# Tiles 5 to 7 in f16 halves, the scan's end column copied by ScalarE, and a new order of the first 480 entries of an attention and MLP kernel

## The chip, the cores and the metric

The kernel runs on one core of one Trainium2 chip. The metric is the device time of one execution in microseconds (us); of several runs the median is taken. The profile is of one further execution.

## The reference

A gated linear attention over 768 steps, for 4 batches of 8 heads of 48 columns, and a layer of two products with a clipped gate between them, on its 3072 outputs of 384 columns.

```python
f = 1.0 / (1.0 + np.exp(-f_logit))
for t in range(S):
    state = f[:, :, t, :, None] * state + np.einsum('bhd,bhe->bhde', k[:, :, t], v[:, :, t])
    y[:, :, t] = np.einsum('bhd,bhde->bhe', q[:, :, t], state)
...
h = x @ w_in
g = h * np.clip(h + 3.0, 0.0, 6.0) / 6.0
return g @ w_out
```

x is y with its heads side by side; w_in is 384 x 2048, w_out 2048 x 384. All is fp32.

## The kernel before

**Work.** The attention is done in 24 units, one for a batch and a chunk of 128 steps. The four units of one chunk make a group of 512 rows for the layer, and there are six groups. The 2048 hidden columns are 16 tiles of 128. Entry mm2.18, for example, is the second product of group 1 (18 = 16 + 2), tile 2.

**A unit.** SP loads its gate logits (`load`, into one of three buffers), its q and k (`loadq`, 512 KB) and v (`loadv`, 200 KB). ScalarE takes the sigmoid (`gate`). VectorE scans the gates backward (`back`, L428), multiplies k by the result (`kmul`, L441), takes the column at which each chunk's scan ends, `sf[:, :, 0]`, and its reciprocal (`rend`: L444 a maximum with a small limit into `ends`, L445 the reciprocal of it), scans forward from the reciprocal over the same buffer (`fwd`, L448), and multiplies q (`qmul`, L454). TensorE transposes k (`tk`, L516), ScalarE copies it out (`ktok`), TensorE makes the update of the state (`kv`, L537), the scores (`att`, L497) and the outputs (`qs`, L571, and `av`, L587). VectorE masks the scores (`mask`, L504), multiplies the old state by `ends` (`decay`, L457) and adds (`carry0`, `carry1`). ScalarE rounds the outputs to f16 into `xmem` (`xh`); TensorE subtracts the rounded part (`xs`) and ScalarE takes the remainder (`xl`), in the first group; a DMA fills the rows between heads (`hole`).

**A weight tile.** SP loads 768 KB (`ld`, into one of three buffers `raws`). ScalarE makes an integer part and a short of its top (`z`, L288; `cy`, L297), VectorE trims, moves and joins it into `wide` (`mid` L301, `dif` L308, `top` L312), ScalarE rounds to f16 (`high`, L317), and the remainder is a subtraction in whole or in halves for w_in and w_out (`low`, `lowi`, `lowo`, L320).

**A tile of the layer.** The first product is nine f16 matmuls of 512 columns: rounded times rounded, remainder times rounded and rounded times remainder, for three blocks of rows (`mm1`, L664). ScalarE makes the clipped part (`relu`), VectorE the gate product (`g`, L678). The second product has two forms. In one it takes g in fp32 and the fp32 weights in `wide`: three matmuls (`mm2x`, L720; for tiles 0 to 4 of group 0 the two halves of 256 rows apart, `mm1a`, `ga`, `mm2a` and so on, L828 to L846). In the other ScalarE rounds g to f16 (`gh`, L683), VectorE or GpSimd takes its remainder (`gl`, L693), and nine f16 matmuls follow (`mm2`, L709). Group 0 uses the fp32 form for tiles 0 to 7, since these come before the remainders of w_out.

**Order.** The program is recorded by walking through a list of entries, `ORDER`; each engine and each DMA queue runs its own instructions in that order. `warm.N` is N idle matmuls of 128 columns on TensorE. A digit after the second dot names a PSUM bank. `ON_POOL` lists the entries that go to GpSimd and not to VectorE. A DMA on SP waits until the one eight before it has landed.

The lines that the change touches:

```python
def turn():
    nc.vector.tensor_scalar_max(ends[:, i], sf[:, :, 0], END_LIMIT)
    nc.vector.reciprocal(rend[:, :, 0], ends[:, i])
def engine(op, i):
    return nc.gpsimd if f"{op}.{i}" in ON_POOL else nc.vector
```

## Time and profile before

| what | us |
|---|---|
| runs shown, three | 458.67, 458.91, 459.29 |
| median | 458.91 |
| the profiled execution | 459.1 |
| its span, first to last instruction | 457.4 |
| TensorE busy | 449.4 |
| VectorE busy | 359.3 |
| ScalarE busy | 231.2 |
| GpSimd busy | 19.0 |

Busy time counts an engine's instructions where at least one runs. Matmuls overlap, and the recorded duration of one goes on to the modelled end of its pipeline. Idle time of an engine stands with what released it. In the stretches that the tables use, the first 480 entries of the list run from the start to about 114 us.

### The profile page before, as it was taken

How to read it: one execution, taken by the hardware profiler on the slowest of the kernel's cores; microseconds unless marked ns; L12 is line 12 of the kernel's file. 1: busy time of each engine (PE TensorE's matmuls, PEld its weight loads, DVE VectorE, ACT ScalarE, POOL GpSimd, SP SyncE). 2: the span in 40 equal slices, each digit the busy share in tenths (PEclk: the TensorE clock that was granted, in tenths of full speed). 3: DMA queues.
4: the chain of work that ended last, by engine and by line, in shares of the span. 5: the costliest groups of instructions: out<-in, count | busy, mean ns of one | idle time of the engine just before them, and what ended most of it. 6: DMA issues, size and time to landing. Idle time of an engine off the chain costs nothing.

```text
span 457.4 us, 12555 instructions
## 1 busy us (share of the span) xinstructions
PE 449.4 (98%) x5445; PEld 292.8 (64%) x5449; DVE 359.3 (79%) x643; ACT 231.2 (51%) x389; POOL 19.0 (4%) x31
## 2 busy tenths in 40 slices
PE   8899999999999999999999999999999999999996
PEld 4578755544455556685767666676676757677764
DVE  6999999979999999989886764888683676466562
ACT  3776777765454445554455265245263443442531
POOL 3000211131000000000000000000000000000000
PEclk9999999999999999999999999999999999999999
DMA  8669656640142512303202240040000010030002
GB/s 283 223 251 385 225 189 251 203 155 16 52 125 99 158 52 59 108 3 120 89 1 85 78 142 18 21 143 2 1 10 1 5 29 2 1 115 2 1 0 73
DMA packets 25531, 43.18 MB, mean 94 GB/s; under 512 B 2560, under 2 KB 17408, under 8 KB 25472
## 3 DMA queue, kind: packets, MB, share of 16 engines
q1 hardware_dynamic: 23872, 41.56, 27.0%
q8 instruction: 43, 0.70, 0.6%
q10 hardware_dynamic: 1600, 0.79, 0.6%
q14 instruction: 16, 0.13, 0.1%
HBM read 36.43 MB, written 4.72 MB: 90 GB/s over the span
## 4 chain that ended last, share of the span: by engine, by line
PE 94%; DVE 2%; DMA 1%; ACT 1%; issue 0%; SPq 0%; ACTq 0%
PE o L709 35%; PE pair L772 16%; PE single L772 9%; PE pair L664 7%; PE single L664 5%; PE o L846 3%; PE pair L497 3%; PE pair L587 3%; PE pair L571 3%; PE pair L537 2%; PE o L720 2%; PE pair L516 2%; PE o_half L862 1%; PE pair L862 1%; PE single L828 1%; PE pair L828 1%
## 5 line engine op out<-in xcount | busy, mean ns | idle before, releaser
L709 PE MATMUL o<-gg,weight 128*128 128x512 f16 x744 | 173.5, 379 | 0.1
L709 PEld LDWEIGHTS <-weight 128*128 128x128 f16 x744 | 71.7, 98 | 73.8
L772 PEld LDWEIGHTS <-weight 128*128 128x128 f16 x672 | 65.1, 98 | 13.3 <-issue 0.2
L772 PE MATMUL pair<-xmem,wide 128*128 128x256 f16 x384 | 51.2, 273 | 0.1
L683 ACT ACTIVATE gg<-raws 128x512 f16<-128x512 f32 x64 | 38.4, 624 | 23.9 <-DVE raws L806 8.1
L772 PE MATMUL single<-xmem,weight 128*128 128x256 f16 x384 | 49.8, 273 | 0.2 <-DVE raws L806 0.2
L801 ACT ACTIVATE raws<-pair,half 128x512 f32<-128x512 f32 x32 | 21.5, 684 | 42.7 <-PE pair L772 33.7
L772 PEld LDWEIGHTS <-wide 128*128 128x128 f16 x384 | 36.9, 98 | 8.7 <-DVE single L787 0.6
L801 ACT ACTIVATE raws<-single,half 128x512 f32<-128x512 f32 x32 | 22.0, 687 | 40.0 <-PE single L772 32.4
L664 PEld LDWEIGHTS <-weight 128*128 128x128 f16 x243 | 23.1, 98 | 26.8 <-issue 0.3
L772 PE MATMUL pair<-xmem,weight 128*128 128x256 f16 x288 | 36.5, 273 | 0.0
L806 DVE SCALAR_TENSOR_TENSOR raws<-raws,single 128x512 f32<-128x512 f32 x32 | 21.8, 682 | 18.4 <-ACT raws L801 18.4
L693 DVE TENSOR_TENSOR gg<-raws,gg 128x512 f16<-128x512 f32 x48 | 31.9, 682 | 5.0 <-ACT gg L683 5.0
L664 PE MATMUL pair<-xmem,weight 128*128 128x512 f16 x144 | 33.2, 379 | 0.0
L787 DVE TENSOR_TENSOR pair<-pair,raws 128x512 f32<-128x512 f32 x16 | 11.2, 697 | 25.5 <-PE pair L772 17.2
L806 DVE SCALAR_TENSOR_TENSOR raws<-raws,pair 128x512 f32<-128x512 f32 x32 | 21.5, 681 | 12.3 <-ACT raws L801 12.1
L448 DVE TENSOR_TENSOR_SCAN suffix<-gates,rend 112x516 f32<-112x516 f32 x24 | 29.7, 1236 | 0.1
L428 DVE TENSOR_TENSOR_SCAN suffix<-gates,unit 112x516 f32<-112x516 f32 x23 | 28.1, 1224 | 0.5 <-ACT gates L422 0.5
L664 PE MATMUL single<-xmem,weight 128*128 128x512 f16 x99 | 23.2, 380 | 0.1
L674 ACT ACTIVATE tg<-pair,half 128x512 f32<-128x512 f32 x16 | 10.9, 687 | 19.5 <-PE pair L664 16.3
L683 ACT ACTIVATE gg<-tg 128x512 f16<-128x512 f32 x24 | 14.4, 626 | 9.1 <-DVE tg L678 5.2
L504 DVE TENSOR_TENSOR a<-pair,causal 128x512 f32<-128x512 f32 x24 | 16.3, 682 | 1.2 <-PE pair L537 1.2
(133 smaller groups left out, 641.6 us busy)
## 6 DMA issues: line engine op xcount, KB each, us to landing
qkf<-qk SPq DMA_DIRECT2D x24, 512.0 KB, 4.9
raws<-w SPq DMA_DIRECT2D x16, 768.0 KB, 6.0
gates<-fg SPq DMA_DIRECT2D x23, 258.5 KB, 3.8
v<-v SPq DMA_DIRECT2D x24, 200.0 KB, 3.8
outT<-os SPq DMA_DIRECT2D x11, 256.0 KB, 3.1
outT<-os SPq DMA_DIRECT2D x8, 128.0 KB, 1.9
wide<-wide SPq DMA_DIRECT2D x32, 24.0 KB, 2.0
outT<-os ACTq DMA_DIRECT2D x2, 256.0 KB, 4.1
```

The lines of the kernel that those rows point to most:

```text
L428: nc.vector.tensor_tensor_scan(flat(sf)[:, ::-1], gt[:, 1:][:, ::-1], flat(unit)[:, ::-1], 0.0, op0=ALU.mult, op1=ALU.add,)
L448: nc.vector.tensor_tensor_scan(flat(sf), gt[:, :NP * (C + 1)], flat(rend), 0.0, op0=ALU.mult, op1=ALU.add,)
L497: nc.tensor.matmul(d["at"][HC * odd:HC * (odd + 1), e, 2 * n + c], t[rs, 1, n, c, odd], t[rs, 0, n, c, odd], start=not growing[at], stop=T ...
L504: nc.vector.tensor_tensor(d["a"].rearrange("r p e t -> r e p t"), d["at"], causal.unsqueeze(1).unsqueeze(1).broadcast_to([128, 2, NP, HC]) ...
L571: nc.tensor.matmul(d["y"][to:to + 64, odd, n, cs], before[rs, p], t[rs, 0, n, c, odd], start=alone and (odd, e) not in seen, stop=False, s ...
L664: nc.tensor.matmul(h, win[:, f, a, k * 128:(k + 1) * 128], g["xt"][:, k, :g["n"] // C, b], start=i == 0, stop=i == 3 * KT - 1,)
L683: nc.scalar.activation(d["gg"][:, 0], d["t"], AF.Copy)
L693: engine("gl", int(g["name"]) * NF + f).tensor_tensor(d["gg"][:, 1], d["t"], d["gg"][:, 0], op=ALU.subtract)
L709: nc.tensor.matmul(g["o"][m], wout[:, f, a, m * 128:(m + 1) * 128], g[f]["gg"][:, b], start=f == 0 and i == 0, stop=f == NF - 1 and i == 2 ...
L772: nc.tensor.matmul(to[:, n * 256:(n + 1) * 256], weights(q, n, a), g["wide"][:, :, block - 3, b], start=fresh and count == 1, stop=count = ...
L801: nc.scalar.activation(to, src, AF.Relu, bias=half, scale=RISE)
L806: nc.vector.scalar_tensor_tensor(to, to, TOP, src, op0=ALU.min, op1=ALU.mult)
```

## The change

Four edits. The second product of tiles 5, 6 and 7 of group 0 goes from `mm2x` to `gh`, `gl` and `mm2`. The maximum in `rend` goes; the reciprocal reads the scan's column itself, and a new entry `ends` copies that column into `ends` on ScalarE. Of the fifteen entries in `ON_POOL` none stays, and `low.8` is new there. The first 480 entries of `ORDER` stand in a new order (494 with the new ones), and after those the order is as before, with `ends.N` ahead of each `rend.N`. Idle matmuls are 47 units in the list, 39 before.

```diff
 ON_POOL = """
-kmul.1 decay.4 kmul.6 lowi.5 kmul.7 decay.7 lowi.7 kmul.8 gl.9 decay.8 gl.11 qmul.8 gl.12 lowo.0 low.14
+low.8
 """.split()
 ORDER = """
-load.0 loadh.0 gate.0 gateh.0 back.0 backh.0 loadq.0 loadv.0 rend.0 kmul.0 load.1 fwd.0 gate.1 back.1 warm.16 tk.0.3
...
+load.0 loadh.0 gate.0 gateh.0 back.0 backh.0 loadq.0 loadv.0 ends.0 rend.0 kmul.0 load.1 gate.1 warm.16 loadq.1 fwd.0
...
+        def close():
+            nc.scalar.activation(ends[:, i], sf[:, :, 0], AF.Copy)
+
         def turn():
-            nc.vector.tensor_scalar_max(ends[:, i], sf[:, :, 0], END_LIMIT)
-            nc.vector.reciprocal(rend[:, :, 0], ends[:, i])
+            nc.vector.reciprocal(rend[:, :, 0], sf[:, :, 0])
...
-            "kmul": kmul, "rend": turn, "fwd": forward,
+            "kmul": kmul, "ends": close, "rend": turn, "fwd": forward,
```

Line numbers of the new kernel are 2 to 4 higher. VectorE, from the first scan of unit 1 on (qkf0 to qkf3 are the q and k of units 0 to 3, `suffix` the scans, `a0` the masked scores; a scan is printed as SCALAR_TENSOR_TENSOR). Before:

```order
L428 SCALAR_TENSOR_TENSOR suffix1_79<-gates1_78,unit_99 112x516
L454 TENSOR_TENSOR qkf0_137<-qkf0_137,suffix0_77 112x512
L444 TENSOR_SCALAR ends_116<-suffix1_79 112x4
L445 RECIPROCAL rend_114<-ends_116 112x4
L504 TENSOR_TENSOR a0_216<-pair0_70,causal_89 128x2x4x64
L448 SCALAR_TENSOR_TENSOR suffix1_79<-gates1_78,rend_114 112x516
L454 TENSOR_TENSOR qkf1_203<-qkf1_203,suffix1_79 112x512
L428 SCALAR_TENSOR_TENSOR suffix2_81<-gates2_80,unit_99 112x516
```

In the changed kernel:

```order
L430 SCALAR_TENSOR_TENSOR suffix1_79<-gates1_78,unit_99 112x516
L458 TENSOR_TENSOR qkf0_137<-qkf0_137,suffix0_77 112x512
L449 RECIPROCAL rend_114<-suffix1_79 112x4
L443 TENSOR_TENSOR qkf1_150<-qkf1_150,suffix1_79 112x512
L452 SCALAR_TENSOR_TENSOR suffix1_79<-gates1_78,rend_114 112x516
L508 TENSOR_TENSOR a0_230<-pair0_70,causal_89 128x2x4x64
L458 TENSOR_TENSOR qkf1_150<-qkf1_150,suffix1_79 112x512
L430 SCALAR_TENSOR_TENSOR suffix0_77<-gates0_76,unit_99 112x516
L430 SCALAR_TENSOR_TENSOR suffix2_81<-gates2_80,unit_99 112x516
```

The maximum of unit 1 is gone, its product of k (kmul.1, on GpSimd before) stands on VectorE, and unit 3's backward scan comes ahead of unit 2's.

SP, from the load of unit 1's gates on (`raws` is a weight tile). Before:

```order
L409 DMA gates1_78<-fg 128x517
L409 DMA gates2_80<-fg 128x517
L413 DMA qkf1_203<-qk 128x1024
L284 DMA raws_74<-w 128x3072
L418 DMA v1_267<-v 128x400
L409 DMA gates0_76<-fg 128x517
L413 DMA qkf2_304<-qk 128x1024
L284 DMA raws_74<-w 128x3072
L413 DMA qkf3_325<-qk 128x1024
L629 DMA xmem_117<-xmem_117 16x3x256 x2
```

In the changed kernel:

```order
L411 DMA gates1_78<-fg 128x517
L415 DMA qkf1_150<-qk 128x1024
L286 DMA raws_74<-w 128x3072
L411 DMA gates0_76<-fg 128x517
L420 DMA v2_193<-v 128x400
L411 DMA gates2_80<-fg 128x517
L420 DMA v1_256<-v 128x400
L415 DMA qkf2_263<-qk 128x1024
L286 DMA raws_74<-w 128x3072 x2
L415 DMA qkf3_327<-qk 128x1024
L633 DMA xmem_117<-xmem_117 16x3x256 x2
```

Unit 3's gates (into buffer 0) now come ahead of unit 2's, v of unit 2 is new among these, and two weight tiles, not one, stand ahead of unit 3's q and k.

ScalarE, from unit 1's first state copy on (`wide` is `z`, `top` is `cy`, xmem with L608 is `xh`, with L620 `xl`). Before:

```order
L550 ACTIVATE middle1_106<-pair1_71 112x2x2x48
L620 ACTIVATE xmem_117<-pair1_71 112x4x128
L557 ACTIVATE state1_111<-pair1_71 112x2x2x48
L608 ACTIVATE xmem_117<-pair0_70 112x4x128
L620 ACTIVATE xmem_117<-pair0_70 112x4x128
L288 ACTIVATE wide_73<-raws_74 128x2x384
L297 ACTIVATE top1_377<-raws_74 128x768
L523 ACTIVATE ktok2_381<-single_72 128x448
```

In the changed kernel:

```order
L554 ACTIVATE middle1_106<-pair0_70 112x2x2x48
L624 ACTIVATE xmem_117<-pair1_71 112x4x128
L446 ACTIVATE ends_116<-suffix2_81 112x4
L561 ACTIVATE state1_111<-pair0_70 112x2x2x48
L290 ACTIVATE wide_73<-raws_74 128x2x384
L299 ACTIVATE top1_340<-raws_74 128x768
L290 ACTIVATE wide_73<-raws_74 128x2x384
L612 ACTIVATE xmem_117<-pair1_71 112x4x128
L446 ACTIVATE ends_116<-suffix0_77 112x4
L527 ACTIVATE ktok2_378<-pair0_70 128x448
L624 ACTIVATE xmem_117<-pair1_71 112x4x128
```

The parts of weight tile 1 and the integer part of weight tile 2 now stand ahead of unit 1's rounding, and the copies of units 2 and 3's end columns are new.

## Rows read from the trace of the kernel before

**Rows 1.** The page: busy time of the engines, and the chain by engine

```profile
PE 449.4 (98%) x5445; PEld 292.8 (64%) x5449; DVE 359.3 (79%) x643; ACT 231.2 (51%) x389; POOL 19.0 (4%) x31
...
PE 94%; DVE 2%; DMA 1%; ACT 1%; issue 0%; SPq 0%; ACTq 0%
```

**Rows 2.** Waits of TensorE, longest in total first: us, times, longest

```profile
PE idle L1071 <- DVE blank L247: 1.1, 1, 1.1
PE pair L497 <- DVE qkf L454: 0.9, 2, 0.7
```

**Rows 3.** Stretches: length, busy us by engine (instructions), clock, DMA share, GB/s

```profile
4.00:18.00 14.00, 12.41 (x276) 7.78 (x278) 12.89 (x21) 6.35 (x13) 1.42 (x1) 1.00 0.87 338
4.00:24.00 20.00, 17.61 (x379) 11.06 (x377) 18.86 (x31) 10.40 (x20) 1.42 (x1) 1.00 0.78 285
24.00:60.00 36.00, 35.69 (x583) 29.30 (x582) 33.65 (x65) 26.70 (x46) 4.40 (x4) 1.00 0.72 270
60.00:114.00 54.00, 54.00 (x621) 27.25 (x620) 47.60 (x77) 38.25 (x56) 10.41 (x10) 1.00 0.47 168
114.00:170.00 56.00, 55.95 (x743) 30.16 (x743) 53.70 (x104) 26.59 (x45) 0.00 (x0) 1.00 0.32 99
```

**Rows 4.** TensorE in order of time, 60 to 80: start, us, line, operation

```profile
67.82 2.74 PE L720 MATMUL o<-tg,wide 128*128 128x512 f32 x6
...
78.94 2.11 PE L709 MATMUL o<-gg,weight 128*128 128x512 f16 x9
```

**Rows 5.** VectorE in order of time, 9 to 28

```profile
9.79 1.16 DVE L444 TENSOR_SCALAR ends<-suffix 112x4 f32<-112x4 f32 x1
...
20.52 0.66 DVE L454 TENSOR_TENSOR qkf<-qkf,suffix 112x512 f32<-112x512 f32 x1
21.09 0.69 DVE L441 TENSOR_TENSOR qkf<-qkf,suffix 112x512 f32<-112x512 f32 x1
21.72 0.36 DVE L301 TENSOR_SCALAR raws<-top 128x768 int16<-128x768 int16 x1
...
27.24 0.42 DVE L841 SCALAR_TENSOR_TENSOR th<-th,single 128x256 f32<-128x256 f32 x1 [0.97 <-ACT th L837]
```

**Rows 6.** GpSimd in order of time, from 4 us on

```profile
9.50 1.42 POOL L441 TENSOR_TENSOR qkf<-qkf,suffix 112x512 f32<-112x512 f32 x1 [5.76 <-DMA qkf<-qk]
```

**Rows 7.** VectorE's groups, 4 to 114: busy us, mean ns, idle before, releaser

```profile
L428 DVE TENSOR_TENSOR_SCAN suffix<-gates,unit 112x516 f32<-112x516 f32 x10 | 12.2, 1225 | 0.5 <-ACT gates L422 0.5
...
L320 DVE TENSOR_TENSOR weight<-wide,weight 128x384 f16<-128x384 f32 x8 | 4.4, 552 | 0.2 <-ACT weight L317 0.2
L441 DVE TENSOR_TENSOR qkf<-qkf,suffix 112x512 f32<-112x512 f32 x6 | 4.1, 687 | 0.3 <-DMA qkf<-qk 0.3
...
L693 DVE TENSOR_TENSOR gg<-tg,gg 128x512 f16<-128x512 f32 x4 | 2.7, 686 | 0.8 <-ACT gg L683 0.7
...
L444 DVE TENSOR_SCALAR ends<-suffix 112x4 f32<-112x4 f32 x9 | 2.4, 271 | 0.1
...
L457 DVE TENSOR_TENSOR decayed<-state,ends 112x192 f32<-112x192 f32 x2 | 0.7, 350 | 0.0
```

**Rows 8.** ScalarE's groups in the same stretch

```profile
L297 ACT ACTIVATE top<-raws 128x768 int16<-128x768 int16 x16 | 14.5, 908 | 0.0
...
L683 ACT ACTIVATE gg<-tg 128x512 f16<-128x512 f32 x10 | 6.1, 626 | 3.1 <-DVE tg L678 3.1
...
L550 ACT ACTIVATE middle<-pair 112x192 f32<-112x192 f32 x4 | 1.3, 330 | 3.2 <-PE pair L537 3.2
```

**Rows 9.** ScalarE in order of time, 2 to 3

```profile
2.98 0.20 ACT L253 ACTIVATE table<-half 128x1 f32<-128x1 f32 x1 [0.89 <-POOL half L251]
```

**Rows 10.** The tile qkf, SP's issues alone, 0 to 12

```profile
L413 SPq DMA_DIRECT2D qkf<-qk x4: 431/432/441, 1.7 to 9.0; - x4
...
  DVE qkf L441: 0.3, 1
...
DMA to landing us min/median/max: 3.8/5.7/9.1
```

**Rows 11.** DMA queues of the whole span: packets, MB, share of 16 engines

```profile
q8 instruction: 43, 0.70, 0.6%
```

More of the change, by code (lines that the diff above doesn't have):

```diff
@@ new lines @@
+ktok.7 top.10 mid.12 gl.7 dif.12 g.8 high.10 low.10 ld.11 gh.8 qs.5.3 qmul.6 z.13 fwd.7 mm2.6 mm2.7 mm1.10.0 relu.9
+loadq.9 relu.10 g.9 ld.15 av.5 gl.8 top.12 att.6.2 gate.8 mm2.8 g.10 mask.6 qs.6.0 cy.13 high.12 qmul.7 gh.9 mid.13
+kv.7.2 gl.9 low.12 xh.5 decay.7 av.6 z.11 dif.13 xh.6 mm1.12.4 xl.5 att.7.1 carry0.7 top.13 gh.10 hole.4 high.13 cy.11
+mask.7 xl.6 low.13 back.8 qs.7.3 mid.11 mm2.9 kmul.8 dif.11 hole.5 relu.12 gl.10 av.7 mm1.13.1 xh.7 ends.8 tk.8.0
+mm2.10 load.9 load.10 top.11 z.15 relu.13 xl.7 ktok.8 hole.6 high.11 kv.8.3 decay.8 g.13 low.11 ld.14 rend.8 gh.13
@@ new lines @@
+qs.17.1 rb.11 qs.16.0 mm2.41 loadq.20 re.11 av.17 xmost.3 loadv.19 av.16 xleast.3 p7.12.3 gbw.11 gh.46 gew.11 xh.16
+gh.45 p1.12.4 ca.12.2 xh.17 gl.45 mm2.42 loadv.23 att.18.1 kv.18.0 decay.18 gh.44 p2.12 p6.12 back.20 gl.46 cs.12
+mm2.43 cx.12.3 carry0.18 gl.44 mask.18 p4.12 ra.12 p5.12 kmul.19 fwd.19 gaw.12 gh.47 mm2.44 decay.19 load.22 ce.12
+loadv.22 od.5 back.21 carry1.18 gl.47 rx.12 qmul.19 p3.12 mm2.45 rb.12 p8.12 mm2.46 kmul.20 re.12 gxw.12 qs.18.0
+gbw.12 gew.12 hole.16 gh.48 p1.13.4 ends.20 rend.20 mm2.47 gate.22 ca.13.2 gl.48 p6.13 hole.17 gh.50 outs.7 av.18
```

174 lines of the change are left out of this document (83 added, 91 removed).

## The prediction

> **What bounds the kernel now.** I read the page's busy line and chain first. TensorE is busy 98% of the span and carries 94% of the chain that ended last [rows 1]; ScalarE is used half the time, GpSimd hardly at all. A busy TensorE can still be a stalled one, so the second view is its waits: the longest two are 1.1 and 0.9 us in total, both at the start of the program, and the list has only smaller ones after them [rows 2]. After the start TensorE runs back to back, and the time is the sum of its work plus what the start loses. The third view is the table by stretch [rows 3]. VectorE is busy 18.86 + 33.65 + 47.60 = 100.1 of the 110 us from 4 to 114, which is the part of the program that the change rearranges, and 53.70 of the 56 us that follow. So there is a second engine close behind the first: 9.9 us of free VectorE time before 114, 2.3 us from 114 to 170. The granted clock is 1.00 in every stretch, so no part of the time is the clock's.
>
> **Part 1: tiles 5 to 7, on TensorE.** The second product of such a tile was three fp32 matmuls of 512 columns (six records): tile 6's takes 2.74 us. Tile 8 already has the form that tiles 5 to 7 get, nine f16 matmuls: 2.11 us [rows 4]. Both numbers hold the same tail of the last matmul, so their difference is what the engine gets back. Three tiles save 3 x (2.74 - 2.11) = 1.9 us, and all of it lies on the engine that sets the end. The price is three roundings to f16 on ScalarE (0.63 us each [rows 8]) and three remainders on VectorE (0.69 us each [rows 7]). ScalarE has idle time for its share; VectorE's share goes into part 3.
>
> **Part 2: the chunk ends.** For each of 24 units VectorE loses the maximum and keeps the reciprocal; ScalarE gains a copy of 112x4. Nine maxima in the window from 4 to 114 take 2.4 us [rows 7]; one of them, at 9.79, took 1.16 us [rows 5], so the others take 0.16 each, 0.2 with the gap behind it. The long one ran while GpSimd was in kmul.1, from 9.50 to 10.92 [rows 6]. It is 1.0 us longer than usual, and I read that as a hold by the neighbour: both the maximum and the GpSimd operation are gone in the new kernel. For the copy there is no row of its shape; the nearest are 128x1 at 0.20 [rows 9] and 112x192 at 0.33 us [rows 8]. I take 0.2, being nearer to one element than to 192, so 24 copies are 5 us (8 at the other end) of ScalarE over the whole span. The cover is ScalarE's idle half. If a copy is late, the second scan of its unit is late next, since that scan overwrites the column that the copy reads; a copy that queues behind a rounding or a weight conversion can be late by up to 0.9 us [rows 8].
>
> **Part 3: fifteen operations leave GpSimd, one goes to it.** In VectorE's durations [rows 7] those that arrive are four kmul and one qmul at 0.69, three decays at 0.35, three half remainders of weights at 0.55, three remainders of g at 0.69: 8.2 us. The long remainder of tile 14 arrives and that of tile 8 leaves, which cancels. With part 1's three remainders (2.1) it is 10.3 us; nine maxima go (2.4). That is 7.9 us more in durations. Neighbours overlap by some 0.08 us (20.52 to 21.09 is 0.57 us for an operation of 0.66 [rows 5]), so seventeen new ones fill 1.4 us less than this, and nine removed free 0.5 us less. The net is 7.0 us of VectorE before 114, against 9.9 us of idle time [rows 3]. It fits, and leaves 2.9 us; of these 0.8 us can't be filled (0.3 at the start for a load [rows 10], 0.5 for a gate [rows 7]). So VectorE allows the first 114 us to shrink by at most 2.1 us before it becomes the bound itself. That is as much as TensorE can gain, so the two engines end up level, and some new waits of TensorE on remainders must be expected. I charge 0.5 us for them (between 0 and 2.6).
> [...]
>
> **Part 4: the start.** Until 26 us VectorE's own row of operations sets the pace, TensorE fills its waits with idle matmuls (39 units before, 47 now; they only fill). I follow the row to kmul.3, which stood at 21.09 [rows 5]. Four maxima are gone, 3 x 0.2 + 1.2 = 1.8 us; kmul.1 is added, 0.6; qmul.2 now stands behind (0.57), one middle step of the weights ahead (0.36, 0.3 with the overlap). Left alone kmul.3 would start at 21.09 - 1.8 + 0.6 - 0.57 + 0.3 = 19.6. But its load is later. The four chunk loads are issued from 1.7 to 9.0, and the slowest, 9.1 us, is this one, issued last: it lands at 18.1 [rows 10]. In the new order of SP the second weight load that now precedes it (768 KB) and one v load (200 KB) go ahead. From 4 to 18 us the queue moved 338 KB a us [rows 3], so these 968 KB put the landing at 18.1 + 2.9 = 21.0. There kmul.3 is only 0.1 us earlier than before, with qmul.2 still to do and the weight step done: level. After that the fifth maximum (0.2) and the idle 0.97 us ahead of the first gate product [rows 5] can go, since that product's matmuls no longer stand behind unit 2's outputs; 0.4 of it I give back, since TensorE then waits on VectorE's longer row. So the start gains 0.7 us. Both ends: the load in time for 19.6 gives 1.3 us more, 2.0 in all; a start that loses 1.5 us is the other, below.
>
> **The sum.** 1.9 + 0.7 - 0.5 = 2.1 us. The profiled execution took 459.1 us, its span 457.4; 459.1 - 2.1 = 457.0. The median of the runs shown is 0.2 us lower, 458.91, so I forecast **456.8 us**, 0.46% faster. From 114 us on the order is the same on all engines but for the ends: VectorE loses fifteen maxima there, ScalarE gains fifteen copies, and TensorE has no wait there that either could shorten. I cost the tail at nothing; its cover is VectorE's 2.3 us of idle time from 114 to 170, and if VectorE leaves the first part late by more, TensorE's remainders are late next.
>
> **Rivals.**
> *VectorE eats it.* The 7.0 us don't pack into the idle time as I suppose, because this idle time sits in a few places: 6.4 of the 9.9 us lie after 60 [rows 3], where VectorE waits for products, while the new work is spread. For it: two engines both over 97% busy that wait for each other. Against it: the moved operations are ready long before they are needed. Time: 2.0 to 2.6 us of new waits, where the other two terms give 2.6; that is 458.3 to 458.9. Chance 0.19.
> *The start goes late (slower).* On ScalarE the conversion of the second new weight block now stands ahead of unit 1's rounding, unit 3's end and the second part of unit 1's tile. ScalarE takes them in order, so a late weight load holds the tile, its copy through DMA and TensorE's first product. That load lands ahead of the 512 KB of kmul.3's, at 21.0 - 1.5 = 19.5 by the same rate, and the conversion ends at 20.4 (0.9 us [rows 8]). I allow 4 us for the rounding, the second part and the copy, 1.5 for the first product and its Relu: the first gate product then runs near 26, against 27.24 [rows 5]. Each us beyond this is nearly a us of the end once these 1.2 us are used up. [...] It decides at a landing after 22.5 or so: the start is then 1.5 us late and the maxima's gain is gone, VectorE's new work finds no room, and with 2.0 us of waits there the time is 458.9 + 1.5 + 2.0 - 1.9 = 460.5. Against it: the 338 KB a us are a mean over 14 us with the queue busy 87% of them, so the estimate has room on its good side too [rows 3]. Chance 0.17.
> *All terms come in.* The load in time, no new waits: 1.9 + 2.0 = 3.9, 455.0 us. Chance 0.20.
> *The reads don't matter.* The order supposes that instruction reads queue behind loads. The trace has 43 reads in the larger of their two queues, together 0.6% of the engines' time [rows 11], and the list of TensorE's waits has none for an instruction [rows 2]. If the supposition is empty, the order holds loads back for nothing; this is a cause of the second rival, with no chance beside it, and it moves no term.
>
> **Numbers.** Forecast 0.44 (456.0 to 457.9), all terms 0.20, VectorE 0.19, late start 0.17. About 0.2%, 0.9 us, is what a measurement of this kernel can tell from no change: faster means under 458.0, slower over 459.8. The first two cases are faster, the third is the same but for a few hundredths, the fourth slower but for as few: 0.65, 0.19, 0.16. The range 454.6 to 459.9 leaves out the better part of the slow case and the best of the good one, about 0.19 together.
>
> **What would show it.** Right: three products of 2.1 us for tiles 5 to 7; no 1.16 us step on VectorE at 10 us; VectorE busy 97% or more from 4 to 112; the first gate product 0.5 to 1 us earlier; TensorE's waits after 30 us at about 0.5 us. Wrong: kmul.3 waiting for its load past 21.5; ScalarE standing idle ahead of a weight conversion at 20 us while unit 1's matmuls are done; a list of TensorE's waits that has VectorE's remainders with 1.5 us or more; or a lower granted clock in the first 30 us.

## The result, and the profile after

The changed kernel takes **462.04 us** (median of five executions, 460.80 to 464.56) against 458.91 (458.67 to 459.29): 1.0077 times as long, 95% interval 1.0062 to 1.0093. It is slower by 3.1 us; 456.8 was forecast, and the range ended at 459.9.

The profiled execution took 460.80 us, the best of the five; its span is 459.0, 1.6 longer than before. In three of the five the mean granted clock was 1.000 (460.80, 461.80, 462.04), in two it was 0.995 and 0.996 (463.54, 464.56).

The page, busy time and chain by engine [rows 1]:

```profile
PE 449.9 (98%) x5474; PEld 294.1 (64%) x5474; DVE 361.6 (79%) x636; ACT 234.9 (51%) x416; POOL 4.7 (1%) x17
...
PE 89%; DVE 8%; DMA 1%; issue 1%; ACT 1%; SPq 0%; ACTq 0%
```

The waits of TensorE (us, times, longest) answer to [rows 2]:

```profile
PE single L832 <- DMA xmem<-xmem: 1.3, 1, 1.3
PE idle L1075 <- DVE blank L249: 1.1, 1, 1.1
PE pair L501 <- issue: 1.0, 1, 1.0
PE o L850 <- issue: 0.6, 1, 0.6
PE pair L616 <- ACT xmem L612: 0.5, 1, 0.5
PE single L668 <- DVE tg L682: 0.5, 1, 0.5
```

The stretches answer to [rows 3]:

```profile
4.00:18.00 14.00, 13.04 (x258) 9.06 (x259) 11.57 (x18) 6.96 (x15) 0.00 (x0) 1.00 1.00 380
4.00:24.00 20.00, 18.88 (x399) 13.22 (x401) 17.07 (x27) 12.63 (x27) 0.00 (x0) 1.00 0.95 349
24.00:60.00 36.00, 33.53 (x493) 26.80 (x484) 33.58 (x64) 28.89 (x52) 0.00 (x0) 1.00 0.77 268
60.00:114.00 54.00, 53.48 (x721) 28.15 (x719) 53.97 (x89) 34.86 (x55) 1.96 (x1) 1.00 0.42 146
114.00:170.00 56.00, 56.00 (x744) 30.16 (x743) 51.40 (x97) 27.36 (x51) 0.00 (x0) 1.00 0.33 99
```

TensorE in order of time; in brackets how long it stood still and for what:

```profile
17.39 0.63 PE L501 MATMUL pair<-qkf 48*64 48x64 f32 x27 [0.96 <-issue]
...
26.52 1.14 PE L832 MATMUL single<-xmem,weight 128*128 128x256 f16 x9 [1.28 <-DMA xmem<-xmem]
...
33.10 0.81 PE L850 MATMUL o<-th,wide 128*128 128x256 f32 x3 [0.64 <-issue]
...
34.84 0.43 PE L616 MATMUL pair<-xmem,less 112*112 112x256 f16 x2 [0.55 <-ACT xmem L612]
...
63.65 2.12 PE L713 MATMUL o<-gg,weight 128*128 128x512 f16 x9
```

But for the 1.1 us ahead of the first matmul the list of waits is new: TensorE stands still twice in the middle of a row of like matmuls with no engine to wait for ("issue"), once for the copies of a finished x tile inside `xmem` (`hole.1`), once behind ScalarE, where `gate.5` holds what follows in that queue for a late load, and once for a gate product. ScalarE and VectorE wait in their turn, behind the first stop for TensorE's scores and then behind the late first product. ScalarE:

```profile
18.14 0.33 ACT L561 ACTIVATE state<-pair 112x192 f32<-112x192 f32 x1 [1.68 <-PE pair L501]
...
32.82 0.63 ACT L424 ACTIVATE gates<-gates 112x512 f32<-112x512 f32 x1 [1.63 <-DMA gates<-fg]
```

VectorE (`kmul.3` at 21.50, the first gate product at 28.21, against 21.09 and 27.24 [rows 5]):

```profile
18.50 0.69 DVE L508 TENSOR_TENSOR a<-pair,causal 128x512 f32<-128x512 f32 x1 [1.60 <-ACT state L561]
...
21.50 0.66 DVE L443 TENSOR_TENSOR qkf<-qkf,suffix 112x512 f32<-112x512 f32 x1
...
28.21 0.42 DVE L845 SCALAR_TENSOR_TENSOR th<-th,single 128x256 f32<-128x256 f32 x1 [1.29 <-ACT th L841]
```

The last rearranged matmuls end at 116.3 us before (not at 114) and at 118.0 in the changed kernel, and from there on the two keep their distance: the Relu of tile 23 (`relu.23`, behind the last rearranged entry) starts at 125.66 before and 127.37 after, the end differs by 1.65. So all is decided before. TensorE's time up to that Relu, added up from its records in the trace (an idle matmul, any other, nothing running; a matmul counts until the next one starts, and the 1.1 us ahead of the first are left out), is the account on which most of what follows rests:

| kernel | relu.23 at | idle matmuls | other work | standing still |
|---|---|---|---|---|
| before | 125.66 | 12.17 | 109.58 | 2.71 |
| changed | 127.37 | 13.93 | 108.12 | 4.12 |
| changed, second trace | 130.12 | 13.72 | 109.95 | 5.25 |
| before, tiles 5 to 7 split (e1) | 127.97 | 13.21 | 108.17 | 5.38 |
| before, ends by ScalarE, placed (e11) | 127.78 | 12.72 | 109.87 | 3.98 |
| changed, 39 idle units (e3) | 126.70 | 11.71 | 107.98 | 5.78 |
| changed, copies first, z.2 later (e13) | 128.25 | 13.83 | 108.51 | 4.69 |
| before, 47 idle units (e17) | 127.32 | 14.13 | 109.21 | 2.77 |
| before, 35 idle units (e18) | 124.85 | 11.42 | 109.68 | 2.54 |

The split is there (other work -1.46), and it is eaten twice: idle matmuls +1.76, standing still +1.41. This is a sum and not yet a cause, since an idle matmul that fills a wait takes from the last column what it adds to the second.

### The profile page after: what moved, and what is told of

Its sections match the earlier page's. It is cut to its first block, busy times and chain, and to the rows that moved or that the text cites. A ratio compares the mean times of both kernels' runs of the same rounds, so it can differ in the third digit from the quotient of the medians.

```text
span 459.0 us, 12603 instructions
## 1 busy us (share of the span) xinstructions
PE 449.9 (98%) x5474; PEld 294.1 (64%) x5474; DVE 361.6 (79%) x636; ACT 234.9 (51%) x416; POOL 4.7 (1%) x17
## 4 chain that ended last, share of the span: by engine, by line
PE 89%; DVE 8%; DMA 1%; issue 1%; ACT 1%; SPq 0%; ACTq 0%
PE o L713 36%; PE pair L776 16%; PE single L776 9%; PE pair L668 7%; PE single L668 4%; PE idle L1075 3%; PE pair L501 3%; PE pair L591 2%; PE pair L575 2%; PE pair L541 2%; PE pair L520 1%; DMA gates<-fg 1%; PE o_half L866 1%; PE pair L866 1%; DVE wide L314 1%
## 5 line engine op out<-in xcount | busy, mean ns | idle before, releaser
L713 PE MATMUL o<-gg,weight 128*128 128x512 f16 x771 | 179.5, 379 | 0.0
L713 PEld LDWEIGHTS <-weight 128*128 128x128 f16 x771 | 74.0, 98 | 76.0
L776 PEld LDWEIGHTS <-weight 128*128 128x128 f16 x672 | 65.1, 98 | 13.3 <-issue 0.2
L668 PEld LDWEIGHTS <-weight 128*128 128x128 f16 x243 | 23.2, 98 | 27.4 <-issue 1.1
L668 PE MATMUL pair<-xmem,weight 128*128 128x512 f16 x153 | 35.3, 379 | 0.0
L668 PE MATMUL single<-xmem,weight 128*128 128x512 f16 x90 | 21.1, 379 | 0.5 <-DVE tg L682 0.5
L687 ACT ACTIVATE gg<-tg 128x512 f16<-128x512 f32 x27 | 16.2, 624 | 8.1 <-DVE tg L682 4.1
```

Of the source, the lines that this page charges most:

```text
L668: nc.tensor.matmul(h, win[:, f, a, k * 128:(k + 1) * 128], g["xt"][:, k, :g["n"] // C, b], start=i == 0, stop=i == 3 * KT - 1,)
L687: nc.scalar.activation(d["gg"][:, 0], d["t"], AF.Copy)
L713: nc.tensor.matmul(g["o"][m], wout[:, f, a, m * 128:(m + 1) * 128], g[f]["gg"][:, b], start=f == 0 and i == 0, stop=f == NF - 1 and i == 2 ...
L776: nc.tensor.matmul(to[:, n * 256:(n + 1) * 256], weights(q, n, a), g["wide"][:, :, block - 3, b], start=fresh and count == 1, stop=count = ...
```

## The experiments

Eighteen runs, with 4 to 11 executions each; one execution of each is traced, and it is not always a typical one. Edits to the order stand as a piece of the list; times are medians with the fastest and the slowest execution, ratios are to the kernel before on the same chip (458.8 to 459.0 each time).

**e1: the split alone.**

```diff
-relu.5 g.5 mm2x.5 cy.7 top.6 high.6 cy.8
+relu.5 g.5 cy.7 gh.5 top.6 gl.5 mm2.5 high.6 cy.8
...
+gh.6 gl.6 mm2.6 lowo.6, gh.7 gl.7 mm2.7 lowo.7 in place of mm2x.6, mm2x.7
```

> The kernel before, with only the split of tiles 5 to 7: gh and gl added, mm2x replaced by mm2, lowo.5 to lowo.7 moved ahead of them; start, chunk ends and GpSimd's operations as before. Theory 1 (the split gains what the rows say and the new start loses more): 458.9 - 1.9 = 457.0, in 456.5 to 457.6, and TensorE's waits as before. Theory 2 (VectorE is what eats the gain): the three remainders (2.1 us) cost TensorE waits, the time stays at 458.3 to 459.3 and waits on VectorE's remainders or gates of 1 us or more stand in TensorE's list between 60 and 114 us.

461.68 (461.27 to 461.87), 1.0059 [1.0046, 1.0072]. Up to relu.5 the trace is that of before to 0.03 us; then TensorE:

```profile
67.31 2.10 PE L664 MATMUL single<-xmem,weight 128*128 128x512 f16 x9 [1.57 <-DVE tg L678]
71.85 2.12 PE L664 MATMUL pair<-xmem,weight 128*128 128x512 f16 x9 [0.49 <-ACT weight L317]
...
77.07 0.69 PE L497 MATMUL pair<-qkf 48*64 48x64 f32 x32 [0.88 <-DVE xmem L622]
```

Other work fell by 1.41, as in the changed kernel, and the three remainders and the output halves, which now come earlier, held a gate product, a rounding and an x tile for more than that. That is theory 2's kind of wait, in a time 2.4 us above its range. It is a matter of places more than of room: VectorE is busy 49.1 of the 54 us from 60 to 114. Of the longest wait 1.0 us is an operation that stood beside GpSimd's `decay.7` and `lowi.7` (64.71 to 66.11) and took 1.69 us where others of its form take 0.69; the gate product stands right behind it.

```profile
64.97 1.69 DVE L454 TENSOR_TENSOR qkf<-qkf,suffix 112x512 f32<-112x512 f32 x1
```

**e2 and e11: the chunk ends alone.** In e2 each copy stands directly ahead of its reciprocal; in e11 three have another place.

```diff
-nc.vector.tensor_scalar_max(ends[:, i], sf[:, :, 0], END_LIMIT)
+nc.scalar.activation(ends[:, i], sf[:, :, 0], AF.Copy)
...
-gate.3 back.3 ... xh.3 mm1a.1 cy.2 xs.3 xl.3 relua.1 z.2 back.4 kmul.4 ends.4 rend.4
+gate.3 ends.2 back.3 ... back.4 ends.4 xh.3 mm1a.1 cy.2 xs.3 xl.3 relua.1 z.2 kmul.4 rend.4
```

> The kernel before, with only the chunk ends changed: VectorE's 24 maxima go, ScalarE copies. kmul.1 is still GpSimd's. Theory 1 (the change of the ends is worth something, at the start): the 1.16 us step at 9.8 us goes, VectorE's row at the start is 1 to 1.8 us shorter, the first gate product comes 0.3 to 1 us earlier; time 458.0 to 458.7. Theory 2 (the copies on ScalarE hold the second scans or the roundings): waits of VectorE on ScalarE's copies, time 459.2 or more. If GpSimd holds whatever stands beside kmul.1, the reciprocal or the next operation takes the extra us instead and the time is 458.9.

> The kernel before with only the chunk ends changed, as in the run that lost 4.9 us, but with three of the copies at another place on ScalarE: units 2 and 4 where VectorE's first scan is just done and no conversion stands ahead, unit 5 behind relub.0. Theory 1 (the loss was the copies' place in ScalarE's order: 0.97 us of ScalarE waiting for a scan, 2.42 us of VectorE waiting for a copy behind a conversion, and the clock that fell after TensorE's 1.84 us): all three waits go and the time is 457.9 to 458.9. Theory 2 (a copy on ScalarE costs more than a maximum on VectorE wherever it stands): 459.2 or more.

e2: 463.64 (462.86 to 464.47), 1.0102 [1.0087, 1.0118]. VectorE, TensorE and the stretches behind show how a copy of 0.2 us costs so much: the second scan of unit 4 waits for a copy that queues behind a conversion on ScalarE, TensorE waits behind that, and the granted clock falls to 0.64 and 0.50 in the 4 us that follow. The clock is not the whole of the loss: the trace is that of the slowest execution (0.993 on the mean), and two others took 462.9 at 1.000.

```profile
34.38 1.23 DVE L452 TENSOR_TENSOR_SCAN suffix<-gates,rend 112x516 f32<-112x516 f32 x1 [2.42 <-ACT ends L446]
```

```profile
35.98 2.38 PE L850 MATMUL o<-th,wide 128*128 128x256 f32 x6 [1.84 <-DVE th L845]
```

```profile
34.00:36.00 2.00, 0.16 (x3) 0.02 (x1) 1.62 (x3) 2.00 (x6) 1.49 (x1) 1.00 0.29 55
36.00:38.00 2.00, 2.00 (x6) 1.42 (x6) 1.93 (x4) 0.91 (x2) 0.00 (x0) 0.64 0.97 370
38.00:40.00 2.00, 2.00 (x65) 1.71 (x64) 2.00 (x4) 0.84 (x1) 0.00 (x0) 0.50 0.97 380
```

In e2 the reciprocal beside `kmul.1` (GpSimd, 8.99 to 10.43) took 0.17 us, so the third forecast fell: the hold that the maximum met did not pass to the next operation.

e11: 459.88 (458.86 to 461.31), 1.0018 [1.0009, 1.0027]. The three waits are gone and 3.8 us with them, but the maxima's 1.8 us of VectorE at the start bring no gain: in the trace, that of the slowest execution, the first Relu is at 27.05 against 26.74, and TensorE stops twice with "issue", 1.6 us in all. The time is one of theory 2's, by stops that neither theory named: the place made nearly all of e2's loss, and the rest did not become a gain.

**e3: 39 idle units in the changed kernel.** Eight single units between 7 and 17 us go.

> The changed kernel with 39 units of idle matmuls as before, in place of 47 (eight single ones out, all of them between 7 and 17 us). Theory 1 (my prediction: idle matmuls only fill): 462.0, no change. Theory 2 (they stand on the path, since TensorE has hardly a gap from 7 to 16 us there): eight units at 0.2 to 0.27 us are up to 2 us, and TensorE reaches mask.1's product earlier; but if the stop at 16.4 us is a late instruction read, that stop gets longer by as much and the time stays within 0.5 us of 462.0.

463.81 (460.08 to 464.65; one more took 467.02), 1.0118 [1.0087, 1.0149]. The profiled execution was the fastest (460.08): both "issue" stops are gone and the first Relu comes 1.0 us earlier, but other waits (copies 2.9 us, a k tile 1.4) more than take their place: standing still grows by 1.7 us in all, and relu.23 is 0.7 us earlier. The other executions had mean clocks of 0.987 to 0.996. Taking the units out of the changed kernel does not give its loss back; why is not decided by this run, since with the units go both their time and their instructions, and the mean clock is lower in most of these executions.

**e4: a fuller queue in the kernel before.**

```diff
-ld.1 carry0.1 ... loadv.3 att.3.2 mask.3 kv.3.1 ld.2
+ld.1 ld.2 carry0.1 ... loadv.3 att.3.2 mask.3 kv.3.1
```

> The kernel before, with one weight load (ld.2, 768 KB) issued directly behind ld.1 as in the changed kernel, all else unmoved. Theory 1 (a fuller load queue makes the instruction reads late): the read that began at 13.8 us begins 0.5 to 1.2 us later, and TensorE, which passed that place with no gap at 16.2 us, stops there for 0.5 to 1.2 us with no other engine named. Theory 2 (the stop in the changed kernel has another cause, the order of its own matmuls): no such stop. In both the chunk load behind it (loadq.3) lands some 2.3 us later, near 20.3, which VectorE reached at 21.1; time 459 to 460 by theory 1, 458.5 to 459.2 by theory 2.

459.18 (458.60 to 461.52), 1.0011 [0.9999, 1.0022]. From 4 to 18 us the queue moved 392 GB/s (338 before, 380 in the changed kernel), and the instruction read began earlier, at 13.07, not later (3.1 us behind the start of the block ahead, 3.4 before); no stop. Theory 1 fell: here the fuller queue did not make the read late.

**e6, e7, e8: one late transfer mended at a time.** e6 puts a weight load behind unit 1's copies, e7 puts `gate.5` behind `relua.2` on ScalarE, e8 does both.

```diff
-loadv.3 ld.3 kmul.3 ... hole.1
+loadv.3 kmul.3 ... hole.1 ld.3
...
-load.5 av.3 loadv.7 gate.5 dif.2 ... att.4.3 relua.2
+load.5 av.3 loadv.7 dif.2 ... att.4.3 relua.2 gate.5
```

> The changed kernel with one weight load (ld.3) issued behind unit 1's copies (hole.1) and not ahead of them; that tile's conversion (z.3) stands behind high.2. Theory 1 (the copies share the queue with 768 KB issued ahead of them): they land within 2.0 to 2.8 us and not 3.1 to 3.5, TensorE's wait of 1.28 us ahead of its first product shrinks to 0.3 to 0.8, and the first Relu comes 0.5 to 1 us earlier than 27.70. Theory 2 (the copies are late because ScalarE hands over the second part at 22.69, and the queue is full in any case): the wait stays over 1.1 us. The time by either is at most 1 us better than the 462.0 of the changed kernel, since later waits follow.

> The changed kernel with ScalarE's gate.5 moved behind relua.2, so that the late gate load (landed at 32.80) holds nothing else on ScalarE; no load is moved. Theory 1 (that one wait, 1.63 us of ScalarE, is passed on to VectorE's ga.1 and TensorE's second gate product mm2a.1): VectorE's idle time of 1.12 us and TensorE's 0.55 us there go, relua.1 stands 1 to 1.6 us earlier than 33.84, and the time is about 1 us better, 461.0. Theory 2 (TensorE's stop at 32.3 us, for an instruction read, sets that place, the gate is hidden behind it): relua.1 earlier, the time unchanged.

> The changed kernel with both moves, the weight load behind unit 1's copies and gate.5 behind relua.2. If the two waits add up: 1.5 to 2 us better than the changed kernel, 460.0 to 460.5, and with the stops below a microsecond no run with a granted clock under 1.00. If the instruction reads and the idle matmuls hold the start as well, under 1 us better.

463.28, 462.74 and 462.36 (1.0094 [1.0079, 1.0109], 1.0075 [1.0053, 1.0098], 1.0078 [1.0064, 1.0093]): none better than the changed kernel's 462.04, which itself became 463.78 in a second run (e16), so that differences of a microsecond or two between these kernels are not clear. e6: the copies took 2.9 to 3.3 us and the wait for them was 1.09, so nearer to theory 2. e7: `relua.1` is 1 us earlier, as said, the time is not; unit 1's copies take 4.2 to 4.7 us, and the next ones, behind two weight loads, up to 6.5:

```profile
27.23 1.14 PE L832 MATMUL single<-xmem,weight 128*128 128x256 f16 x9 [2.39 <-DMA xmem<-xmem]
...
40.08 2.08 PE L832 MATMUL single<-xmem,weight 128*128 128x256 f16 x9 [2.18 <-DMA xmem<-xmem]
```

The "issue" stop near 17 us was in all three, 1.2, 0.6 and 0.5 us long.

**e10, e13, e14: all copies ahead of the weight loads.** e13 adds one move on ScalarE, e14 also takes the eight idle units out.

```diff
-ld.1 ld.2 ... hole.0, ld.3 ... hole.1 ... load.5 ... ld.5 ... hole.2 hole.3
+ld.1 ... hole.0 ld.2, hole.1 ... load.5 ld.3 ... hole.2 hole.3 ld.5
```

> The changed kernel with every pair of tile copies ahead of the weight load that SP issued just before it: ld.2 behind hole.0, ld.3 behind load.5, ld.5 behind hole.3, with z.2 and z.3 later on ScalarE to match, and gate.5 behind relua.2. Theory 1 (the copies wait in the queue behind 768 KB loads, and the three kernels that moved one thing only handed the wait on to the next pair of copies): the copies land within 1.9 to 2.8 us of their issue, TensorE's waits for them (1.3 in the changed kernel, 2.4 to 4.6 with one thing moved) fall under 0.8 in sum, and the time is 458.5 to 460.5. Theory 2 (the queue's total bytes set the start, whatever their order): another wait of 1 us or more takes their place (late weights or chunk loads), and the time stays at 461.5 or more.

> As the run with the copies first, with one more move on ScalarE: z.2 behind cy.2, so that ktok.3 and the matmuls behind it do not wait for a weight load that was asked for late (1.56 us of ScalarE, 2.2 us of TensorE in that run). Theory 1 (the new start loses by places in ScalarE's and SP's order alone): TensorE's waits from 7 to 45 us fall under 1 us in sum, the clock stays at 1.00, relua.0 comes near 27 us, and the time is 457.5 to 459.5. Theory 2 (a wait removed is handed to the next in a start whose queue is 85 to 100% busy): another wait of 1 us or more in TensorE's list, 461 or more.

> As the run before it in this call, with 39 idle units in place of 47. Theory 1 (the eight units stand on the path once the waits are gone): 1 to 1.8 us faster than with 47. Theory 2 (TensorE waits instead, and the granted clock falls in some executions, as in the changed kernel with 39): no faster in the median, and executions with a mean clock below 0.997 among them.

462.13 (461.43 to 463.33), 461.52 (460.65 to 464.23) and 460.95 (459.53 to 462.63); 1.0074 [1.0059, 1.0089], 1.0064 [1.0043, 1.0085], 1.0048 [1.0030, 1.0066]. The copies now cost TensorE 0.4 us in e10 and 0.2 in e13, but not because they are faster: unit 1's pair takes 3.6 to 3.9 us from issue to landing in e10 and 3.4 to 3.8 in e13, where theory 1 asked for 1.9 to 2.8 and the changed kernel has 3.1 to 3.5, and it lands at 25.96 and 26.61 (26.43 there). TensorE comes to it later, held by something else: in e10 a conversion waits for the weights now loaded later, and TensorE waits 2.2 us behind it; in e13 that is mended, and a v load and an instruction read come last:

```profile
25.13 0.91 PE L541 MATMUL pair<-v,ktok 64*64 64x48 f32 x48 [1.12 <-DMA v<-v]
...
33.81 0.81 PE L850 MATMUL o<-th,wide 128*128 128x256 f32 x3 [1.20 <-issue]
```

Theory 2 holds for the sum: TensorE stands still 4.4 to 4.7 us in each of the three. e14 is the best of the mended ones, 1.1 us under the changed kernel's first median and 2.8 under its second (e16, on the same chip, where the ranges do not meet), with two of eight executions at a clock of 1.00. Against e13 the eight units are worth 0.6 us, less than theory 1 said, and the ranges overlap.

**e5, e9, e12: the start of before, then the rest of the new order.** The first 147 entries of before, then the changed kernel's; e9 mends the seam of e5, e12 is e9 with the old `ON_POOL`.

```diff
-kv.4.2 cy.4 z.4 ... relub.0 ... relub.2
+kv.4.2 ... relub.0 ... relub.2 ... high.3 z.4 cy.4 gb.2 mid.4 dif.4 top.4
```

> The start of the kernel before (its first 147 entries, to some 35 us, with VectorE's maxima for units 0 to 4, GpSimd's kmul.1 and 39 idle units), then the changed kernel's order with its split tiles, ScalarE's chunk ends and VectorE in place of GpSimd. At the seam gate.6, back.6, mm1a.2 and lowi.2 stand later than in the changed kernel, so that no engine waits for what the new start would have done already. Theory 1 (the new start loses 2.7 us in the profiled runs, and the rest of the new order gains about 1 us on the old): 457.0 to 458.5, and the first gate product as before. Theory 2 (the rest of the new order gains nothing, VectorE being busy 53.97 of 54 us from 60 to 114): 459 or more, with waits of TensorE on VectorE of over 2 us after 35 us.

> As the run with the old start, but with the seam mended: tile 4's conversions stand behind relub.2, as in the kernel before, so that ScalarE no longer waits 4.3 us for weights that the old start had not yet asked for. Theory 1 (the new start loses, the rest of the new order gains about 1 us on the old): TensorE has no wait above 1 us behind 7 us, the clock stays at 1.00, and the time is 457.0 to 458.5. Theory 2 (the rest of the new order needs the work that the new start does early): TensorE waits 2 us or more for weights or remainders between 40 and 60 us, and the time is 459.5 or more.

> As the mended run with the old start, with GpSimd keeping the fifteen operations that it had in the kernel before. Theory 1 (VectorE is nearly full from 60 to 114 us, 53.97 of 54, so the fifteen operations cost what VectorE has not got): 0.5 to 2 us faster than with VectorE doing them. Theory 2 (an operation on GpSimd takes twice as long and is late for the matmul or holds the neighbour, which is why it was worth moving): 0.5 us or more slower, with TensorE's waits on GpSimd in its list.

463.96, 461.63 and 463.25 (1.0110 [1.0096, 1.0125], 1.0058 [1.0044, 1.0073], 1.0089 [1.0073, 1.0106]). In e5 ScalarE waits at the seam for weights that the old start had not asked for, TensorE 3.55 us behind it, and the clock is 0.50 from 42 to 46:

```profile
40.35 0.88 ACT L289 ACTIVATE wide<-raws 128x768 int32<-128x768 uint32 x1 [4.32 <-DMA raws<-w]
```

e9 has two waits of the same kind left in its trace (its slowest execution), 1.6 and 2.0 us. So these runs don't show what the rest of the new order is worth with an old start: inconclusive for that. With GpSimd keeping its fifteen operations the time is 1.6 us longer, but the executions overlap (460.69 to 464.85 and 461.71 to 463.92); in its trace half a weight remainder on VectorE takes 2.65 us, 0.55 elsewhere, beside GpSimd's operations of 99.31 to 101.64, and the gate product behind it is 1.17 us late for TensorE.

**e15: tiles 6 and 7 split in the kernel before, GpSimd doing the remainders.**

```diff
-z.8 decay.7 ... lowi.7 ... mm2x.6 ... mm2x.7
+z.8 gh.6 decay.7 ... lowi.7 gl.6 lowo.7 ... mm2.6 ... gh.7 gl.7 ... att.7.2 mm2.7
```

> The kernel before with tiles 6 and 7 split and tile 5 as it was; GpSimd, idle for most of 56 to 81 us, does their remainders (gl) and their weights' output halves (lowo), ScalarE the roundings in its idle time, the second product of tile 7 behind att.7. Theory 1 (the split gains 0.47 to 0.63 us a tile wherever its remainder is ready): 457.6 to 458.3. Theory 2 (GpSimd's 1.17 us for a remainder is too late, or its work holds VectorE): TensorE waits for gl or lowo by 0.5 us or more, and the time is 458.7 or more.

463.69 (462.56 to 464.78), 1.0105 [1.0088, 1.0123]. One wait took it:

```profile
76.25 0.69 PE L498 MATMUL pair<-qkf 48*64 48x64 f32 x32 [3.28 <-DVE xmem L623]
```

`att.7`, which now stands ahead of `mm2.7`, needs the bank of unit 5's outputs, and VectorE's `xl.5`, which frees it, is late. Ahead of it VectorE's operations beside GpSimd's were held three times: 1.42 us for 0.55 (66.79), 1.62 for 1.02 (68.24), 0.94 for 0.16 (74.46). The time is theory 2's, and so is the hold; the wait that it ended in was not named.

**e16: the changed kernel again.**

> The changed kernel unaltered, for a second trace. If TensorE's stops for instruction reads are a matter of each execution, the stop of 0.96 us at 16.4 us and that of 0.83 us at 32.3 us come out different by some tenths or are gone, while the waits for the copies (1.3) and behind gate.5 stay; if they belong to the order, they are as they were to 0.2 us. Time 461 to 464.6 by either.

463.78 (463.51 to 464.05, four executions, mean clocks 0.991 to 0.996), 1.0108 [1.0093, 1.0122]. Waits and stretches:

```profile
PE single L832 <- DMA xmem<-xmem: 1.4, 1, 1.4
PE pair L616 <- ACT xmem L612: 1.3, 1, 1.3
PE pair L501 <- issue: 1.2, 1, 1.2
```

```profile
34.00:36.00 2.00, 0.63 (x5) 0.45 (x6) 1.47 (x3) 2.00 (x5) 0.00 (x0) 1.00 0.83 346
36.00:38.00 2.00, 2.00 (x7) 1.64 (x8) 2.00 (x4) 2.00 (x4) 0.00 (x0) 0.55 0.33 115
38.00:40.00 2.00, 2.00 (x11) 1.38 (x10) 1.45 (x3) 0.33 (x1) 0.00 (x0) 0.60 0.12 26
```

The stops stand at the same places and differ in length (0.96 and 1.24; 0.64 and 0.1): place by the order, length by the execution. The wait behind `gate.5` is 1.31 here, 0.55 in the first trace; the clock then falls to 0.55, and other work is 1.83 us longer than in the first trace (109.95 against 108.12). This explains a part of the changed kernel's spread: in this trace the clock falls behind the waits of the start, in the first, at 1.00 throughout, it does not.

**e17 and e18: idle units in the kernel before.** Eight more behind the operations where the changed kernel has them; four fewer (the `warm.4` behind `high.0`).

```diff
-xh.0 kmul.1 tk.1.4
+xh.0 warm.1 warm.1 kmul.1 tk.1.4
...
-mid.1 high.0 warm.4 kv.2.1
+mid.1 high.0 kv.2.1
```

> The kernel before with eight more single idle units (47 in place of 39), put behind the same operations as in the changed kernel: one behind tk.0's, two behind qmul.0, one ahead of av.0, two behind xh.0, two behind xl.0; nothing else is moved. Theory 1 (my prediction: they only fill the waits): 458.9 within 0.4. Theory 2 (they stand on the path, at 0.22 us each): 459.8 to 460.7, with the first Relu 0.8 to 1.8 us later than 26.74 and smaller waits of TensorE ahead of it.

> The kernel before without the four idle units (one matmul of 512 columns, 1.12 us at 21.86) that stand ahead of unit 2's key-value product; kv.2's input is ready at 22.1, and it ran at 22.91. Theory 1 (idle units on the path cost what they last): kv.2, the first gate product and VectorE's ga.0 (0.97 us idle ahead of it) come 0.5 to 0.8 us earlier, 458.1 to 458.5. Theory 2 (VectorE's row of operations sets the first gate product, the units only fill): 458.9. Theory 3 (without them the granted clock falls behind the 0.7 us wait at 21.2 us): executions with a mean clock below 0.997, 459.5 or more.

e17: 460.74 (460.10 to 462.22), 1.0049 [1.0034, 1.0064]. This run shows what idle units can cost. The first Relu is at 26.77, 0.03 us from before, but that is luck: the executions begin with loads that land at different times (VectorE's first product of k, which waits for one, runs at 5.58 in before and at 6.58 in e9). Counted from TensorE's first key-value product, the first Relu comes 18.2 to 18.3 us later in before, e4, e5, e9 and e12, which share the start, 17.9 in e1 and e15, and 18.7 here. So 0.4 to 0.8 us of the eight units' time (8 x 0.22) gets there; the rest fills, and TensorE's standing still up to there falls from 2.57 to 1.02. The time is the one that theory 2 gave (460.7), but less than half of it comes in the way that theory 2 said. Then, 14 us behind the last added unit, in the middle of a product whose twin ran without a gap before:

```profile
31.14 0.59 PE L847 MATMUL o<-th,wide 128*128 128x256 f32 x2
33.34 1.02 PE L847 MATMUL o<-th,wide 128*128 128x256 f32 x4 [1.61 <-issue]
```

and the distance to before is 1.6 to 1.7 us from there to the end.

e18: 458.43 (457.48 to 459.37, eleven executions), 0.9994 [0.9985, 1.0003]. The first Relu is 0.9 us earlier, and 17.6 us behind the first key-value product where it was 18.2; the end of the trace is 0.7 earlier. So these four units cost some time, as in theory 1. The interval takes in no change; it is the only kernel here with a median below that of before.

**The stops.** The larger instruction queue has 43 reads of 16,384 bytes [rows 11], and TensorE 10,950 records before (all but 56 of them matmuls and weight loads) and 11,008 in the changed kernel, 255 and 256 for a read, so I take these reads for TensorE's; the stops lie at the 449th, 961st and 1217th record, give or take one, which are 256 or 512 apart; a block here is 256 records. (One more "issue", 0.33 us at 95.53 in e12, is none of these: TensorE's sequencer waits there for a semaphore until 95.48.) For some traces, the block that begins at the 449th and at the 1217th: when TensorE began the block ahead, when it had come to the end of that, when the read ran, when it went on, and the stop by the list of waits.

```
kernel              begins  at end  read            goes on  stop
block at 449
before               10.44  16.18   13.79 to 14.75   16.21   -
changed              11.06  16.43   15.00 to 15.99   17.39   0.96
changed, 2nd trace   10.86  16.22   14.87 to 15.96   17.46   1.24
e4  (fuller queue)    9.96  15.69   13.07 to 14.04   15.46   -
e18 (35 units)       10.19  15.71   13.61 to 14.60   16.03   0.32
block at 1217
before               27.36  34.63   30.08 to 31.03   34.37   -
changed              27.84  32.46   30.68 to 31.62   33.10   0.64
e13 (copies, z.2)    27.98  32.61   31.45 to 32.42   33.81   1.20
e17 (47 units)       27.16  31.73   30.96 to 31.94   33.34   1.61
```

In every one of these stops TensorE goes on 1.39 to 1.50 us after its read has ended. In these rows a block is gone through in 4.6 to 7.3 us, and from its beginning to the point where the next can run (the end of a stop, or 1.4 us after the read) it takes 5.1 to 6.6. So a block full of a unit's small matmuls (48 of them in the 0.91 us of a key-value product) is used up sooner than the next one arrives. At 449 the kernel before resumed 1.46 us after its read, as the stopped ones do. It stood over the edge already: between two starts of like matmuls, otherwise 0.01 us apart, lie 0.24 us, and the 48 matmuls of that product take 1.14 us where the next unit's take 0.91. The list of waits, which goes by the modelled ends, has 0.02 us there.

```profile
15.51 1.14 PE L537 MATMUL pair<-v,ktok 64*64 64x48 f32 x48
...
22.91 0.91 PE L537 MATMUL pair<-v,ktok 64*64 64x48 f32 x48
```

## Why the prediction was wrong

**The step that failed** is part 4, "So the start gains 0.7 us". The first gate product came 0.97 us later than before and not 0.5 to 1 earlier, and at relu.23 the profile is 1.7 us behind in spite of the split. Two terms of that part were wrong. The first is "idle matmuls (39 before, 47 now; they only fill)", put at nothing. As time the eight fill for the most part: in e17 0.4 to 0.8 of their 1.8 us reach the first Relu. As instructions they cost more: eight units are 32 records more, they shift every later block of 256 against the work, and in e17 a stop of 1.61 us comes of it; both together are 1.9 us in the median. In the changed kernel the two stops are 1.60 of the 4.12 us that TensorE stands still; in e3, without the eight units, both are gone. That the stops' place comes from the count is shown by e17. The second is the 4 us allowed for unit 1's tile, which took 5.5 (below).

How the 3.1 us divide is not shown. With the stops gone e3 has relu.23 only 0.7 us earlier and no better median, since other waits take their place, and no kernel that mended one or several places of the new start came under 460.95, 1.9 us above before. Why the read of block 449 begins 2.8 us after the block ahead in one kernel (e3) and 4.0 in another (e16) is open too: the fullest queue (e4) had 3.1.

**The rival "the reads don't matter"** was held to move no term. I read it from a share (0.6% of the engines' time [rows 11]) and from a list of waits without a read [rows 2]. Both were true, and neither shows a margin; here there was none, with 0.24 us already lost. By count such a stop is rare, with at most two for 43 reads in a trace; in the rows above those that come cost 0.32 to 1.61 us.

**The start otherwise.** The dates that I worked out were near: ld.2 landed at 19.53 (19.5), q and k of unit 3 at 20.97 (21.0), kmul.3 ran at 21.50 (level with 21.09). The first gate product was 0.97 us late instead of 0.5 to 1 early. I had allowed 4 us from the end of the conversion (20.89) for rounding, second part and copy; it was 5.5, to 26.43: the copies were issued at 22.72, behind a 768 KB load issued at 18.95, and took 3.1 to 3.5 us against 2.3 to 2.8 before. That this load made them late is not shown: with it behind them they took 2.9 to 3.3 (e6), and with the weight loads moved as in e10 and e13 3.4 to 3.9. The waits for them that shrank there came back elsewhere (2.22 us in e10, 1.12 and 1.20 in e13).

**Part 1** had the right place and was mis-sized a little: 2.74 became 2.12 us for each of the three, and other work fell by 1.46 (1.41 in e1), not 1.9, as TensorE's account counts it. **Part 2**: a copy took 0.19 to 0.21 us in the trace, 0.2 was taken. The price of a late copy, named as what is late next, was met in e2: 2.42 us, where up to 0.9 had been named. The hold by the neighbour is borne out: the maximum beside `kmul.1` took 1.15 to 1.16 us in e1, e5, e12 and e15 too. It is met again in the changed kernel, by the one operation that goes to GpSimd (`low.8`):

```profile
61.52 1.96 POOL L322 TENSOR_TENSOR weight<-wide,weight 128x768 f16<-128x768 f32 x1 [57.78 <-ACT weight L319]
```

```profile
61.88 1.82 DVE L461 TENSOR_TENSOR decayed<-state,ends 112x192 f32<-112x192 f32 x1
```

The product for the old state takes 0.33 to 0.35 us elsewhere; here it ends 0.2 us after GpSimd, and from it VectorE runs without a gap to the gate product for which TensorE stands still 0.52 us. Part 3 let `low.8` and `low.14` cancel and had no term for this 1.5 us. What it is worth is not shown, since no run changes it alone. **Part 3**: from 4 to 114 VectorE's busy time rose by 4.5 us, to 104.6, and not by 7.0, although two halves (`lowo.5`, `lowo.7`) that stood behind 114 now stand ahead of it, which the list had missed; which of its terms were too large is open. VectorE is busy 53.97 of 54 us from 60 to 114, so that its idle time, 5.4 us, lies ahead of 60, and TensorE waits 0.5 us on it; 0.5 had been charged. The rival "VectorE eats it" is not what happened in the changed kernel; in e1, without the new order, it is.

**The slow rival** had the sign and 460.5, from another mechanism: ScalarE never stood ahead of z.2, and the landing that was to decide (22.5) was at 19.53; that the profiled execution took 460.80 is luck. Of the four signs that were to show the forecast wrong none appeared in the profile: I had looked for late data and not for late instructions. Of the five that were to show it right the first two came; VectorE was busy 95% from 4 to 112 and not 97, the first gate product was late, and TensorE's waits after 30 us were 1.7 us and not 0.5.

**Profile and median.** By the profiled execution the loss is 1.7 us, by the median 3.1. The forecast took the granted clock as settled, 1.00 in every stretch of [rows 3]. In e16 it is 0.55 and 0.60 from 36 to 40 us, behind a wait of 1.31, and other work is 1.8 us longer. This does not explain the median: that execution (462.04) and a third (461.80) ran at 1.000 and are 1.0 to 1.2 us above the profiled one. Stops that differ in length from one execution to the next, as in e16, may be what they lost; no trace shows it.

Four things stay open: how the loss divides between the stops, the copies and the waits behind them; what makes the copies slow; what the later part of the new order is worth by itself (e5 and e9 broke at the seam); and what delays a read.

## What to carry to other kernels

Count TensorE's instructions, not their time alone: where a program starts with many small matmuls, find in the trace where each block of records ends (256 here) and how long ahead its read was in, and treat anything that adds or moves instructions, idle ones too, as a change to those margins. A wait taken out can go to the next one in line: in seven kernels that mended the changed kernel's start TensorE stood still for 4.4 to 6.1 us, against 4.1 and 5.2 in the two traces of the unmended one. Compare medians of several executions: the changed kernel's profiled one was its best. When a wait for a transfer shrinks, look at the transfer's own time before calling it mended. And look at what VectorE runs beside an operation handed to GpSimd: here one such product took 1.82 us, 0.33 to 0.35 elsewhere.
